# Attention planned with other durations for transfers, landings, query splits and GpSimd steps

## The chip, the cores and the metric

The kernel runs as one program on one core of one Trainium2 chip. The metric is the device time of one execution in microseconds (us), the median of several runs. Every tensor is fp32.

## The reference

Attention with a position bias from a small network, then a mixture of 8 experts of which each token takes 2, then a two-layer network with a cosine gate. Cut to what matters:

```python
# attention: B=2, H=8, S=576, D=64; hidden width 32 of the bias network
scores = q @ k.T / sqrt(D)
x = log1p(|i - j|) / log1p(max(i, 1))
bias = relu(x[..., None] @ w1 + b1) @ w2
attn = exp(scores + bias - max); attn /= sum + 1e-9
x = (attn @ v).transpose(0, 2, 1, 3).reshape(1152, 512)
# experts: 1152 tokens, top 2 of 8, 512 -> 1024 -> 512
noisy = x @ w_gate + log1p(exp(x @ w_noise)) * noise
out[mask] += top2_w[mask, k, None] * (relu(x[mask] @ w1[e]) @ w2[e])
# last stage: 512 -> 2048 -> 512
h = x @ w_in
return (h * cos(h)) @ w_out
```

## The kernel before

The program has two stages under one launch: attention with the routing of the tokens (0 to about 246 us of the span), and the experts with the last network (the rest). Matrix products keep fp32 exactness by splitting an operand in a rounded high part and a low part, so most products run twice.

**Attention** works in 72 steps. A step is one head of one block of 128 query rows. The first 8 steps are the block `it=4` (the last 64 rows of both batches), and steps 8 to 71 are `it=0` to `it=3` for either batch, 8 heads each. One step is: four score matmuls into `S` (L489, eight in the first block), a DVE operation that adds the bias and takes the row minimum (`ttr`, L494, which writes `t` and `m`), the exponential on ACT (L503), four transposes on PE (L510), and a copy `et` to SBUF (L275 on ACT or L277 on DVE). Every second step adds a transpose of the two 64-column tails (L522) and its copy `etl`, and the product with `vt` (`av`, L538). `S` has two buffers, so the scores of step n+2 wait for the `ttr` of step n.

Around that stand the jobs that feed it. `qjobs` (L289) loads a query block (L308), copies its high part (`qt`, L305 on ACT or L307 on DVE) and subtracts for the low part (L316, DVE). `kjobs` does the same for the keys (L329, low part L339 on DVE or GpSimd). `vjobs` loads the values, four transfers of 512 KB from L283. `bjobs` makes the bias of `it=4` and `it=0`: features (L381, L383), matmuls (L392), evacuations `bst` (L398 on ACT, L400 on DVE) and a transfer into the tile `bias` (L404). `bjobs2` makes the bias of `it=1` to `3` from the table `dtab` (loaded into the tile `kraw` at L926, scaled at L925), with features L428 and L430, matmuls L438, evacuations L448 and L450, a transfer to `dist` in DRAM (L458) and one back (L462). After the last head of a block the routing of its 128 tokens is worked out (a tile, 0 to 8; its one-hot and slot arithmetic on DVE between L786 and L857, its scatter on GpSimd).

**What sets the order.** Nothing is scheduled on the chip. Every operation is handed to `Plan.op` with the engines it may run on and a duration for each, a priority, and what it reads and writes. `Plan.run` (L67 on) simulates this with one clock per engine: it takes, among the operations that could start within 0.08 us of the earliest, the one of lowest priority, gives it to the engine where it would end soonest, and emits it. A transfer with `xfer` occupies one modelled DMA pipe for so long and counts as landed `land` us after that. So the numbers handed over decide both which engine does a piece of work and where it stands in that engine's queue. On the chip every engine works through its queue strictly in that order and waits where data are not there. SP issues all loads and stores of this stage from one queue too. The second stage has a plan of its own, with `land=2.3`.

The four `vt` transfers are planned together, after the last key loads (`after=[kl[...]]`), and every `av` reads all of `vt`.

Of the kernel before, what the change touches and what calls it, by code (L numbers as in the profile page):

```python
# [165 lines left out]
def attention_moe_cosine_mlp_kernel(  # L166
# [5 lines left out]
    nc = tc.nc  # L172
# [53 lines left out]
    with ExitStack() as actx:  # L226
# [39 lines left out]
        P = Plan(bufs, ("aux",))  # L266
# [20 lines left out]


        def qjobs(it, b, prio, after=()):  # L289
            key = (it, b)  # L290
            n = 128 if it < 4 else 64
            o = 0 if it < 4 else 64 * b

            def raw():
                return tl("qraw", key).bitcast(F32).rearrange("p h s -> p (h s)")[:, 0:H * n]

            def rows16():
                return raw().rearrange("p (h a r) -> p h a r", h=H, r=16)

            def part(u):  # L300
                return tl("qt", key)[:, u, :, o:o + n].rearrange("p h (r a) -> p h a r", r=16)

            def hi(e):
                if e == "ACT":
                    nc.scalar.activation(part(0), rows16(), AF.Copy)  # L305
                else:
                    nc.vector.tensor_copy(part(0), rows16())  # L307
            P.op({"SP": 0.45}, lambda e: nc.sync.dma_start(  # L308
                raw(), qd[b][:, it * 1024:it * 1024 + 8 * n]),
                prio - 3, w=[("qraw", key)], xfer=0.0115 * n, after=after)  # L310
# [15 lines left out]
        def kjobs(p, b, prio):  # L326
# [3 lines left out]
                           w=[("kraw", key)], xfer=0.82, after=late)  # L330
            for j in range(2):
# [11 lines left out]
                P.op({"DVE": 0.67, "POOL": 1.5}, lo, prio + 0.2, r=[("kraw", key), ("kt", key, j, 0)], w=[("kt", key, j, 1)])  # L343
# [21 lines left out]
        def bjobs(it, when):  # L365
            nA = 8 if it < 4 else 4
            for a in range(nA):
# [35 lines left out]
                for d in range(2 if it == 4 else 1):  # L403
                    bdma[a if it == 4 else 10 + a] = P.op({"SP": 0.625}, (lambda d, a, key: lambda e: nc.sync.dma_start(  # L404
                        spread(tl("bias", it), it, a, d), tl(*key)[:, 0:S]))(d, a, key),
                        pr + 0.2, r=[key + (0,), key + (1,)], w=[("bias", it, a, d)], xfer=0.82)
# [6 lines left out]
        def bjobs2(it, when):  # L413
            for a in range(8):
# [38 lines left out]
                for side in range(2):  # L453
# [7 lines left out]
                    w=[("dist", A)], xfer=0.85)  # L461
# [3 lines left out]
                    pr + 0.3, r=[("dist", A)], w=[("bias", it, a, 0)], xfer=0.82)  # L465
# [14 lines left out]
        def ajobs(n):  # L480
# [20 lines left out]
            qks[n] = P.op({"PE": 0.25 * 2 * len(bs)}, qk, n, r=nin, w=[("S", n)])  # L501
# [16 lines left out]
            P.op({"DVE": 0.1, "POOL": 0.34}, lambda e: (nc.gpsimd if e == "POOL" else nc.vector).tensor_copy(  # L518
# [20 lines left out]
            P.op({"PE": 1.34 if b is not None else 2.1}, av, n + 3, r=["v", ets[0], ets[1], el], w=[ax2], hold=[ok])  # L539
# [8 lines left out]
        def wjobs(i, pr):  # L548
            rk = ("raw", i)
            P.op({"SP": 0.45}, lambda e: nc.sync.dma_start(tl(*rk), mwp[i]), pr, w=[rk], xfer=1.46,  # L550
# [329 lines left out]
        def setup():  # L880
            P.op({"SP": 0.45}, dma(sm1, small1), -20, w=["sm1"], xfer=0.5)
            P.op({"SP": 0.45}, dma(w1l, ltab), -20, w=["w1l0"], xfer=1.64)
# [620 lines left out]
```

## Time and profile before

| | us |
|---|---|
| median of three runs | 681.82 |
| lowest, highest | 681.18, 684.20 |
| the profiled execution | 689.02 |
| its span (first to last instruction) | 687.2 |
| end of attention (last matmul of L657) | 245.88 |
| PE busy of the span | 632.1 (92%) |
| DVE busy of the span | 510.0 (74%) |

The profiled execution is 7.2 us longer than the median of the runs. Times below are positions in its span. PE is the busiest engine over the span. The rows that matter for this case come from the first 246 us.

### The profile page before, as it was taken

Reading aid. Unit: us, or ns where it says so; the run is one execution under the profiler, and the core shown is the slowest. Engines: PE = TensorE matmul, PEld = TensorE weight load, DVE = VectorE, ACT = ScalarE, POOL = GpSimd, SP = SyncE. Lnnn points to the kernel's source line nnn. Section 1 sums busy time; section 2 is a strip of 40 time slices with the busy share of each in tenths; the row PEclk is TensorE's granted clock in tenths of the full one; section 3 lists DMA queues with packets and bytes.
Section 4 is the critical chain, followed back from the end, with each engine's and each line's share of the span. In section 5 each row is a group of like instructions: output and inputs, shape, how many; then the busy total and the mean of one; then the engine's idle time right before and its main releaser. Section 6 shows DMA issues by size and latency. Waiting matters only on the chain.

```text
span 687.2 us, 12766 instructions
## 1 busy us (share of the span) xinstructions
PE 632.1 (92%) x4678; PEld 552.3 (80%) x4678; DVE 510.0 (74%) x1271; ACT 395.6 (58%) x791; POOL 107.1 (16%) x179
## 2 busy tenths in 40 slices
PE   5778998898899849999998998999999999999996
PEld 1346676675578649999998998999999999999996
DVE  6796897898878637989969888766998545554443
ACT  5666687777668525666645646544665444444333
POOL 4140124313222210002100011021400040001000
PEclk9998999999999959999999999999999999999999
DMA  5858788676658329698897897974730040001001
GB/s 174 207 162 255 247 281 270 214 217 199 204 165 267 106 73 279 189 302 269 238 301 211 250 281 207 250 201 157 240 100 25 0 138 1 1 7 40 1 1 46
DMA packets 58177, 116.45 MB, mean 169 GB/s; under 512 B 7024, under 2 KB 26864, under 8 KB 56048
## 3 DMA queue, kind: packets, MB, share of 16 engines
q1 hardware_dynamic: 54544, 104.41, 51.1%
q0 software_dynamic: 3552, 11.04, 4.8%
q8 instruction: 41, 0.67, 0.4%
q14 instruction: 40, 0.33, 0.2%
HBM read 78.12 MB, written 32.58 MB: 161 GB/s over the span
## 4 chain that ended last, share of the span: by engine, by line
PE 51%; DMA 6%; DVE 5%; issue 2%; ACT 1%; SPq 0%; DVEq 0%; POOL 0%; ACTq 0%
PE H L1002 25%; PE Y L1002 25%; DMA wraw<-in_mwp_dram 3%; DMA io<-xg 2%; DVE qt L1042 1%; DVE whl L1042 1%; DVE io L1153 1%; DMA xg<-x,token 1%; PE H L1191 1%; DMA bias<-xg 1%; DVE s L1072 1%; DVE s L1103 0%; ACT qt L1040 0%; DVE hhl L1133 0%; DVE qraw L1108 0%
## 5 line engine op out<-in xcount | busy, mean ns | idle before, releaser
L1002 PE MATMUL Y<-hhl,qt 128*128 128x304 f32 x468 | 73.3, 302 | 4.3 <-DVE hhl L1133 4.1
L1002 PE MATMUL Y<-w,hhl 128*128 128x512 f32 (+1 forms) x330 | 74.8, 372 | 0.0
L1002 PEld LDWEIGHTS Y<-hhl,qt 128*128 128x128 f32 x468 | 66.8, 188 | 5.6 <-DVE hhl L1133 5.5
L1002 PEld LDWEIGHTS Y<-w,hhl 128*128 128x128 f32 x330 | 56.7, 188 | 8.7
L503 ACT ACTIVATE e<-t,m 128x576 f32<-128x576 f32 x72 | 55.5, 771 | 11.8 <-DVE m L494 10.6
L489 PE MATMUL S<-kt,qt 128*128 128x288 f32 x320 | 59.0, 313 | 2.9 <-DVE m L494 2.9
L494 DVE CUSTOM_DVE_ANT_0 t<-S,bias 128x576 f32<-128x576 f32 x72 | 53.4, 750 | 9.4 <-DMA bias<-e 2.7
L1002 PE MATMUL H<-qraw,qt 128*128 128x304 f32 (+1 forms) x300 | 50.9, 321 | 8.3 <-issue 8.3
L1002 PEld LDWEIGHTS H<-qraw,qt 128*128 128x128 f32 x300 | 47.9, 199 | 9.1 <-issue 8.6
L489 PEld LDWEIGHTS S<-kt,qt 128*128 128x128 f32 x320 | 45.1, 190 | 8.5 <-DVE m L494 4.1
L1131 ACT ACTIVATE hhl<-H 128x304 fp32r<-128x304 f32 x64 | 26.7, 417 | 40.3 <-PE H L1002 38.4
L1002 PE MATMUL H<-qraw,w 128*128 128x384 f32 x264 | 49.3, 336 | 0.0
L1242 ACT ACTIVATE u<-H 128x384 f32<-128x384 f32 (+1 forms) x52 | 23.8, 466 | 42.2 <-PE H L1002 40.3
L1002 PEld LDWEIGHTS H<-qraw,w 128*128 128x128 f32 x264 | 46.6, 188 | 1.7
L510 PE MATMUL etp<-ident,e 128*128 128x128 f32 x288 | 44.6, 278 | 3.3 <-ACT e L503 2.6
L538 PE MATMUL aux<-et,vt 128*64 128x128 f32 (+1 forms) x640 | 42.5, 277 | 5.5 <-DMA vt<-in_vd_dram 3.2
L1042 DVE TENSOR_TENSOR qt<-wraw,qt 128x1024 fp32r<-128x1024 f32 x35 | 42.7, 1224 | 6.2 <-ACT qt L1040 5.6
L1002 PE MATMUL Y<-hhl,whl 128*128 128x304 f32 x300 | 45.6, 300 | 0.0
L1248 ACT ACTIVATE u<-u 128x384 f32<-128x384 f32 (+1 forms) x52 | 25.7, 498 | 34.1 <-DVE u L1246 33.8
L538 PEld LDWEIGHTS aux<-et,vt 128*64 128x64 f32 x640 | 33.2, 143 | 13.7 <-DMA vt<-in_vd_dram 3.5
L1254 DVE TENSOR_TENSOR hhl<-u,hhl 128x384 fp32r<-128x384 f32 (+1 forms) x52 | 27.2, 526 | 22.7 <-ACT hhl L1252 22.0
L1040 ACT ACTIVATE qt<-wraw 128x1024 fp32r<-128x1024 f32 x36 | 37.7, 1053 | 10.5 <-DMA wraw<-in_mwp_dram 6.1
(206 smaller groups left out, 1372.6 us busy)
## 6 DMA issues: line engine op xcount, KB each, us to landing
wraw<-in_mwp_dram SPq DMA_DIRECT2D x64, 512.0 KB
r<-in_mw2p_dram SPq DMA_DIRECT2D x16, 1024.0 KB
dist<-bst SPq DMA_DIRECT2D x24, 295.5 KB
bias<-dist SPq DMA_DIRECT2D x24, 288.0 KB
xg<-zero SPq DMA_DIRECT2D x20, 256.0 KB
yd<-zero SPq DMA_DIRECT2D x20, 256.0 KB
yd<-io SPq DMA_DIRECT2D x32, 160.0 KB
io<-xg SPq DMA_DIRECT2D x28, 160.0 KB
```

Source lines behind the costliest of these rows:

```text
L489: nc.tensor.matmul(s[:, hf, 0:HF], tl("qt", (it, bb))[:, u, h, :], kt[:, bb, h, hf * HF:hf * HF + HF], start=(i == 0), stop=(i == len(term ...
L494: nc.vector.tensor_tensor_reduce(out=tl("t", n).rearrange("p (a j) -> p a j", a=2), in0=tl("S", n)[:, :, 0:HF], in1=tl("bias", it)[:, h, : ...
L503: P.op({"ACT": 0.76}, lambda e: nc.scalar.activation(tl(*ek)[:, 0:S], tl("t", n), AF.Exp, bias=tl("m", n), scale=-1.0, accum_out=tl("rs", ...
L510: nc.tensor.transpose(tl("etp", n)[:, j * 128:(j + 1) * 128], tl(*ek)[:, j * 128:(j + 1) * 128], ident)
L538: nc.tensor.matmul(tl(*ax2)[h0, q0], lw, rx, start=(s == 0), stop=(s == 4))
L1002: nc.tensor.matmul(out_, lw(a), rx(b_), start=(first and i == 0), stop=(last and i == n - 1))
L1040: P.op({"ACT": 0.947}, lambda e: nc.scalar.activation(wt(i)[:, 0], tl(*rk), AF.Copy), pr, r=[rk], w=[wname(i) + (0,)])
L1042: P.op({"DVE": 1.135, "POOL": 2.4}, lambda e: (nc.gpsimd if e == "POOL" else nc.vector).tensor_tensor(wt(i)[:, 1], tl(*rk), wt(i)[:, 0].bi ...
L1131: P.op({"ACT": 0.053 + 0.00083 * W}, lambda en: nc.scalar.activation(tl(*hk)[:, 0, 0:W], tl(*pk)[:, 0:W], AF.Relu), g + 0.3, r=ks, w=[hk + ...
L1242: P.op({"ACT": 0.06 + 0.00083 * m}, lambda e: nc.scalar.activation(u(), h(), AF.Copy, scale=1.0 / (2.0 * math.pi), bias=0.25), z, r=ks, w= ...
L1248: P.op({"ACT": 0.187 + 0.00083 * m}, lambda e: nc.scalar.activation(u(), u(), AF.Sin, scale=2.0 * math.pi), z + 0.04, r=[un[1]], w=[un[2]])
L1254: P.op({"DVE": 0.069 + 0.00104 * m}, lambda e: nc.vector.tensor_tensor(part(1), u(), part(0).bitcast(F32), op=OP.subtract), z + 0.07, r=[u ...
```

## The change

Only numbers that the attention plan is fed are changed, and none of the code that an operation emits. Transfers get longer times, a landed transfer counts 2.0 us after its pipe time where it was 1.25 us, the query split costs become larger on either engine (high part for 128 rows: ACT 0.92 to 1.90 us, DVE 0.60 to 0.94; low part on DVE 1.14 to 2.01), and two GpSimd steps, the scores and the products with `vt` get other durations. The `av` of the first block falls from 2.1 to 1.4 us.

```diff
-        P = Plan(bufs, ("aux",))
+        P = Plan(bufs, ("aux",), land=2.0)
...
+        QA, QD, QL = 0.0144, 0.0068, 0.0152
...
-                prio - 3, w=[("qraw", key)], xfer=0.0115 * n, after=after)
+                prio - 3, w=[("qraw", key)], xfer=0.0133 * n, after=after)
...
-            P.op({"ACT": 0.0067 * n + 0.06, "DVE": 0.0042 * n + 0.065}, hi, prio + 0.1, r=[("qraw", key)],
+            P.op({"ACT": QA * n + 0.06, "DVE": QD * n + 0.065}, hi, prio + 0.1, r=[("qraw", key)],
                  w=[("qt", key, 0)])
-            P.op({"DVE": 0.0084 * n + 0.065}, lambda e: nc.vector.tensor_tensor(
+            P.op({"DVE": QL * n + 0.065}, lambda e: nc.vector.tensor_tensor(
...
-                           w=[("kraw", key)], xfer=0.82, after=late)
+                           w=[("kraw", key)], xfer=1.17, after=late)
...
-                P.op({"DVE": 0.67, "POOL": 1.5}, lo, prio + 0.2, ...
+                P.op({"DVE": 0.68, "POOL": 1.65}, lo, prio + 0.2, ...
...
-                     xfer=1.46, after=[kl[tuple(VAF[s])]] if VAF[s] else [])
+                     xfer=1.7, after=[kl[tuple(VAF[s])]] if VAF[s] else [])
...
-            P.op({"PE": 1.34 if b is not None else 2.1}, av, n + 3, ...
+            P.op({"PE": 1.38 if b is not None else 1.4}, av, n + 3, ...
```

In the same way the transfers of `bias` go from 0.82 to 1.18, of `dist` from 0.85 to 1.01, of the first expert weights from 1.46 to 1.7 and of the feature table from 1.64 to 2.08; scores go from 0.25 to 0.265 per batch and half, and the GpSimd copy of a tail from 0.34 to 0.40.

The emitted instructions are the same kinds in nearly the same number, in another order and partly on another engine, and only in the attention stage. Of the eight high parts of queries with 128x1024 elements, ACT copies 6 before and 1 now, DVE 2 and 7. Copies `et` go from 14 to 12 on DVE, tail copies of scores from 14 to 13, output copies from 10 to 8, and ACT takes these. Of the low parts of the keys GpSimd takes 8 where it took 9. Lines from 287 on have a number that is one higher in the changed kernel.

**Place 1, start of the stage.** The queue of SP, from the next to last key load on, before:

```order
L329 DMA kraw<-in_kd_dram 128x576
L404 DMA bias<-bst 16x8x576 x2
L329 DMA kraw<-in_kd_dram 128x576
L404 DMA bias<-bst 16x8x576
L283 DMA vt<-in_vd_dram 128x1024 x4
L926 DMA kraw<-in_dtab_dram 128x512
L404 DMA bias<-bst 16x8x576
L308 DMA qraw<-in_qd_dram 128x1024 x2
```

And after:

```order
L330 DMA kraw<-in_kd_dram 128x576
L405 DMA bias<-bst 16x8x576
L330 DMA kraw<-in_kd_dram 128x576
L405 DMA bias<-bst 16x8x576
L283 DMA vt<-in_vd_dram 128x1024 x4
L405 DMA bias<-bst 16x8x576
L927 DMA kraw<-in_dtab_dram 128x512
L309 DMA qraw<-in_qd_dram 128x1024 x2
L405 DMA bias<-bst 16x8x576
```

The four `vt` transfers stand behind the sixth `bias` transfer of `it=0` instead of the seventh, and the eighth has gone behind the two query loads.

DVE at the same place before, from the evacuation ahead of the first query block of `it=0` on (`ISA t,m` is the `ttr` of step 4):

```order
L400 TENSOR_SCALAR bst<-aux,sm_73 128x288
L307 CAST qt<-qraw 128x8x8x16
L383 TENSOR_SCALAR feat<-w1l,sm_73 128x576
L316 TENSOR_TENSOR qt<-qraw,qt 128x8x8x16
L494 ISA t,m<-S,bias 128x576
L494 ISA m 128x1
L277 CAST kt<-kraw 64x576
L400 TENSOR_SCALAR bst<-aux,sm_73 128x288
```

And after:

```order
L277 COPY et<-etp 128x512
L495 ISA t,m<-S,bias 128x576
L495 ISA m 128x1
L308 CAST qt<-qraw 128x8x8x16
L384 TENSOR_SCALAR feat<-w1l,sm_73 128x576
L317 TENSOR_TENSOR qt<-qraw,qt 128x8x8x16
L277 CAST kt<-kraw 64x576
L401 TENSOR_SCALAR bst<-aux,sm_73 128x288
```

The `ttr` of step 4 has moved ahead of the query split.

**Place 2, the first steps of `it=2`.** PE before, from the scores of step 41 on:

```order
L489 MATMUL S<-kt,qt 128x288 x4
L510 MATMUL etp<-ident,e_2125 128x128 x4
L438 MATMUL aux<-feat,sm_73 32x400 x4
L522 MATMUL aux<-ident,e_2095 128x128
L489 MATMUL S<-kt,qt 128x288 x8
L510 MATMUL etp<-ident,e_2234 128x128 x4
```

And after, from the same scores:

```order
L490 MATMUL S<-kt,qt 128x288 x4
L539 MATMUL aux<-et,vt 64x128 x8
L539 MATMUL aux<-etl,vtl 64x128 x2
L439 MATMUL aux<-feat,sm_73 32x400 x4
L511 MATMUL etp<-ident,e_2168 128x128 x4
L523 MATMUL aux<-ident,e_2086 128x128
L539 MATMUL aux<-et,vt 64x128 x8
L539 MATMUL aux<-etl,vtl 64x128 x2
L439 MATMUL aux<-feat,sm_73 32x416 x4
L719 MATMUL aux<-ot,sm_74 32x128 x4
L737 MATMUL aux<-ident,ot 128x128 x4
L490 MATMUL S<-kt,qt 128x288 x8
```

Between the scores of step 41 and of step 42 stand two `av`, two bias matmuls and the first part of a routing tile; before there were one set of transposes, one bias matmul and a tail.

**Place 3, the routing of the last tile but one.** DVE before, from the `ttr` of step 71 on:

```order
L559 TENSOR_TENSOR qt<-wraw,qt 128x512 x2
L797 TENSOR_SCALAR rt<-rt 128x2
L799 TENSOR_TENSOR rt<-rt 128x1
L824 ISA rt<-oh,aux 128x8
L824 ISA rt 128x1
L824 ISA rt<-oh,aux 128x8
L824 ISA rt 128x1
L277 COPY et<-etp 128x512
L828 TENSOR_TENSOR rt<-rt 128x2
```

And after:

```order
L798 TENSOR_SCALAR rt<-rt 128x2
L800 TENSOR_TENSOR rt<-rt 128x1
L495 ISA t,m<-S,bias 128x576
L495 ISA m 128x1
L560 TENSOR_TENSOR qt<-wraw,qt 128x512 x2
L825 ISA rt<-oh,aux 128x8
L825 ISA rt 128x1
L825 ISA rt<-oh,aux 128x8
L825 ISA rt 128x1
L856 TENSOR_SCALAR rt<-rt 128x1
L829 TENSOR_TENSOR rt<-rt 128x2
```

The copy `et` has gone from the middle of this arithmetic (to ACT), and the two small steps for the weights stand ahead of the `ttr`.

## Rows read from the trace of the kernel before

**Rows 1.** Windows: stretch, length, busy PE, PEld, DVE, ACT, POOL, clock, DMA, GB/s
```profile
40.00:49.00 9.00, 6.71 (x56) 3.89 (x53) 8.94 (x14) 6.55 (x13) 5.01 (x4) 1.00 0.35 98
49.00:54.00 5.00, 4.10 (x34) 2.87 (x31) 4.87 (x8) 2.44 (x5) 1.27 (x2) 1.00 0.85 279
54.00:61.00 7.00, 3.77 (x41) 2.97 (x41) 1.67 (x7) 1.69 (x4) 0.25 (x2) 0.85 1.04 306
61.00:66.00 5.00, 5.00 (x65) 4.22 (x62) 4.07 (x10) 4.61 (x8) 0.00 (x0) 0.52 0.71 253
...
66.00:229.00 163.00, 151.28 (x1566) 112.96 (x1564) 140.10 (x526) 122.57 (x293) 43.84 (x115) 1.00 0.70 218
120.00:160.00 40.00, 35.30 (x361) 25.92 (x361) 36.10 (x145) 28.89 (x69) 11.89 (x31) 1.00 0.69 216
```

**Rows 2.** Timeline of PE, start of the stage: start, us, what, wait ahead
```profile
48.41 1.10 PE L392 MATMUL aux<-feat,sm 128*32 128x288 f32 x6 [1.63 <-DVE bst L400]
...
57.08 0.34 PE L538 MATMUL aux<-et,vt 128*64 128x64 f32 x4 [0.76 <-DMA vt<-in_vd_dram]
59.89 0.48 PE L538 MATMUL aux<-et,vt 128*64 128x64 f32 x4 [2.48 <-DMA vt<-in_vd_dram]
...
62.17 1.12 PE L538 MATMUL aux<-et,vt 128*64 128x64 f32 x16
...
66.98 0.69 PE L538 MATMUL aux<-et,vt 128*64 128x64 f32 x16
```

**Rows 3.** Timeline of SP's queue, the same stretch
```profile
48.42 0.54 SPq L404 DMA_DIRECT2D bias<-bst  x1
49.01 2.15 SPq L283 DMA_DIRECT2D vt<-in_vd_dram  x4
51.81 0.33 SPq L926 DMA_DIRECT2D kraw<-in_dtab_dram  x1
```

**Rows 4.** Timeline of DVE, the same stretch
```profile
42.78 1.09 DVE L307 CAST qt<-qraw 128x1024 fp32r<-128x1024 f32 x1
43.71 0.49 DVE L383 TENSOR_SCALAR feat<-w1l,sm 128x576 f32<-128x576 f32 x1
44.12 2.15 DVE L316 TENSOR_TENSOR qt<-qraw,qt 128x1024 fp32r<-128x1024 f32 x1
46.12 0.75 DVE L494 CUSTOM_DVE_ANT_0 t<-S,bias 128x576 f32<-128x576 f32 x1
...
47.84 0.52 DVE L400 TENSOR_SCALAR bst<-aux,sm 128x288 f32<-128x288 f32 x1
...
60.67 0.49 DVE L925 TENSOR_SCALAR kraw<-kraw,sm 128x512 f32<-128x512 f32 x1 [4.24 <-DMA kraw<-in_dtab_dram]
```

**Rows 5.** Timeline of ACT, the exponential of step 4
```profile
46.97 0.78 ACT L503 ACTIVATE e<-t,m 128x576 f32<-128x576 f32 x1 [0.80 <-DVE m L494]
```

**Rows 6.** Timeline of PE and DVE at the first steps of it=1 and it=2
```profile
100.73 0.77 PE L438 MATMUL aux<-feat,sm 128*32 128x336 f32 x8
...
111.63 0.75 DVE L494 CUSTOM_DVE_ANT_0 t<-S,bias 128x576 f32<-128x576 f32 x1
...
156.33 0.76 DVE L494 CUSTOM_DVE_ANT_0 t<-S,bias 128x576 f32<-128x576 f32 x1 [0.76 <-DMA bias<-dist]
...
157.15 1.49 PE L489 MATMUL S<-kt,qt 128*128 128x288 f32 x8 [1.33 <-DVE m L494]
```

**Rows 7.** Groups by line and shape, 0 to 246 us: count, busy, mean ns
```profile
L305 ACT ACTIVATE qt<-qraw 128x1024 fp32r<-128x1024 f32 x6 | 12.7, 2116 | 0.6 <-PE S L489 0.4
...
L277 DVE COPY et<-etp 128x512 f32<-128x512 f32 x14 | 9.5, 680 | 0.1
...
L307 DVE CAST qt<-qraw 128x1024 fp32r<-128x1024 f32 x2 | 2.2, 1106 | 0.0
```

**Rows 8.** Timeline of DVE and PE at the end of the stage
```profile
229.86 0.69 DVE L277 COPY et<-etp 128x512 f32<-128x512 f32 x1
...
254.18 2.11 PE L1002 MATMUL H<-qraw,qt 128*128 128x304 f32 x7 [8.31 <-issue]
```

More of the change, by code (lines that the diff above doesn't have):

```diff
@@ L342, in kjobs @@
                 P.op(cost(S, False), hi, prio + 0.1, r=[("kraw", key)], w=[("kt", key, j, 0)])
-                P.op({"DVE": 0.67, "POOL": 1.5}, lo, prio + 0.2, r=[("kraw", key), ("kt", key, j, 0)], w=[("kt", key, j, 1)])
+                P.op({"DVE": 0.68, "POOL": 1.65}, lo, prio + 0.2, r=[("kraw", key), ("kt", key, j, 0)], w=[("kt", key, j, 1)])
         def knames(p, b):
@@ L405, in bjobs @@
                         spread(tl("bias", it), it, a, d), tl(*key)[:, 0:S]))(d, a, key),
-                        pr + 0.2, r=[key + (0,), key + (1,)], w=[("bias", it, a, d)], xfer=0.82)
+                        pr + 0.2, r=[key + (0,), key + (1,)], w=[("bias", it, a, d)], xfer=1.18)
         dist = {}
@@ L460, in bjobs2 @@
                     tl("bst", key)[:, 0:591]))(A, key), pr + 0.2, r=[("bst", key, 0), ("bst", key, 1)],
-                    w=[("dist", A)], xfer=0.85)
+                    w=[("dist", A)], xfer=1.01)
                 P.op({"SP": 0.625}, (lambda A, a: lambda e: nc.sync.dma_start(
@@ L464, in bjobs2 @@
                     dist[A][15:15 + 128 * BW].rearrange("(r h w) -> r h w", r=16, h=8)[:, :, 0:S]))(A, a),
-                    pr + 0.3, r=[("dist", A)], w=[("bias", it, a, 0)], xfer=0.82)
+                    pr + 0.3, r=[("dist", A)], w=[("bias", it, a, 0)], xfer=1.18)
         def bnames(it):
@@ L500, in ajobs @@
             nin = [x for bb in bs for x in qnames(it, bb) + knames(h // 2, bb)]
-            qks[n] = P.op({"PE": 0.25 * 2 * len(bs)}, qk, n, r=nin, w=[("S", n)])
+            qks[n] = P.op({"PE": 0.265 * 2 * len(bs)}, qk, n, r=nin, w=[("S", n)])
             P.op({"DVE": 0.67}, ttr, n + 0.5, r=[("S", n)] + bnames(it), w=[("t", n), ("m", n)])
@@ L517, in ajobs @@
             e0 = ("e0", n // 2)
-            P.op({"DVE": 0.1, "POOL": 0.34}, lambda e: (nc.gpsimd if e == "POOL" else nc.vector).tensor_copy(
+            P.op({"DVE": 0.1, "POOL": 0.4}, lambda e: (nc.gpsimd if e == "POOL" else nc.vector).tensor_copy(
                 tl(*e0)[:, S:S + 64], tl(*ek)[:, 512:S]), n + 1.5, r=[ek], w=[e0 + ("tail",)], shy={"DVE": 0.6})
@@ L538, in av @@
                             nc.tensor.matmul(tl(*ax2)[h0, q0], lw, rx, start=(s == 0), stop=(s == 4))
-            P.op({"PE": 1.34 if b is not None else 2.1}, av, n + 3, r=["v", ets[0], ets[1], el], w=[ax2], hold=[ok])
+            P.op({"PE": 1.38 if b is not None else 1.4}, av, n + 3, r=["v", ets[0], ets[1], el], w=[ax2], hold=[ok])
             P.op(cost(128), lambda e: cp(tl(*ok)[:, p, :], tl(*ax2)[:, 0:128], e), n + 3.2, r=[ax2], w=[ok + (p,)])
@@ L549, in wjobs @@
             rk = ("raw", i)
-            P.op({"SP": 0.45}, lambda e: nc.sync.dma_start(tl(*rk), mwp[i]), pr, w=[rk], xfer=1.46,
+            P.op({"SP": 0.45}, lambda e: nc.sync.dma_start(tl(*rk), mwp[i]), pr, w=[rk], xfer=1.7,
                  after=[qks[min(int(pr), NS - 1)]])
@@ L881, in setup @@
             P.op({"SP": 0.45}, dma(sm1, small1), -20, w=["sm1"], xfer=0.5)
-            P.op({"SP": 0.45}, dma(w1l, ltab), -20, w=["w1l0"], xfer=1.64)
+            P.op({"SP": 0.45}, dma(w1l, ltab), -20, w=["w1l0"], xfer=2.08)
             P.op({"DVE": 0.7}, lambda e: nc.vector.tensor_scalar(w1l, w1l, w1c, None, op0=OP.mult), -20,
```

## The prediction

> **What bounds the kernel now.** I read the table of windows first. From 66 to 229 us PE is busy 151.28 of 163 us and DVE 140.10 [rows 1]: PE sets the pace there, with DVE not far behind, and from 120 to 160 us DVE is even the fuller one (36.10 of 40 against 35.30). The start is another matter. From 40 to 54 us DVE is full (8.94 of 9, 4.87 of 5) and PE waits for it; from 54 to 61 us nearly everything stands still: PE 3.77 of 7, DVE 1.67, ACT 1.69, while the DMA engines are at 1.04 of their share [rows 1]. Just before, from 40 to 49 us, those same DMA engines are at 0.35. So transfers that could have run in the idle stretch are bunched in the next one.
>
> Next I read the timelines of the start for what ends each wait. PE has two waits for `vt`, 0.76 and 2.48 us, and goes on at 59.89 [rows 2]. DVE waits 4.24 us for the table `dtab`, until 60.67 [rows 4]. SP's queue says why both are late: `vt` is issued at 49.01, right behind the seventh `bias` transfer at 48.42, and `dtab` at 51.81 behind `vt` [rows 3]. That `bias` transfer waits for the evacuation that DVE does from 47.84 to 48.36 [rows 4], and SP issues in order. Nothing that `vt` itself needs is late; it is queued behind something that is.
>
> The waits have a second price. In the window 61 to 66 us the granted clock is 0.52, the lower of the two levels (1.2 GHz), and it is 1.00 from 66 us on [rows 1]; 16 `av` matmuls take 1.12 us at 62.17 and 0.69 us at 66.98 [rows 2].
>
> **The change part by part.** The profiled execution is 689.02 us for a span of 687.2; I make the sum against it and carry the difference over to the median of the runs, 681.82. The rows are about 1% long for that, which is nothing beside the bounds.
>
> *`vt` one place earlier.* It now waits behind the sixth `bias` transfer. That hangs on an ACT evacuation that stands behind the exponential of step 4 (46.97 [rows 5]), and so on the `ttr` of step 4. This `ttr` has moved ahead of the query split on DVE: by starts, 46.12 − 42.78 = 3.34 us for the copy, a feature and the subtraction [rows 4]. The exponential could begin at 43.6, end with the rest of its operation near 44.6, the evacuation near 45.1, and `vt` go out near 45.8 instead of 49.01: −3.2 us. If ACT finds other work ahead of it, or the sixth bias matmul waits for a feature, it is less; below nothing it can't be, since the seventh transfer is behind it in either order.
>
> *What PE makes of it.* The last part of `vt` would be there at 59.89 − 3.2 = 56.7. PE reaches its first `av` some 0.7 earlier (one copy `et` of 680 ns [rows 7] is now behind the `ttr` of step 7, on which the scores ahead of `av` hang), so it would wait some 0.7 us instead of 0.76 + 2.48 = 3.24. PE: −3.2 us, bounds −1 (the transfer shares the DMA engines with others and comes hardly earlier) and −3.9.
>
> *What DVE makes of it.* The seventh `bias` transfer still waits for the same evacuation, since the work ahead of it on DVE is the same in another order, so `dtab`, now right behind that one alone, goes out near 49.0 instead of 51.81: −2.8, and the 4.24 us of idle time shrink to near 1. But then the order has two things that DVE did not have there: a tail copy that waits for PE to get through four sets of `av`, 1.3 to 3.3 us of waiting by whether these run at the upper or lower clock level, and both query copies, 2 × 1106 ns where ACT did one in 2116 [rows 7]. Against the 4.24 and the 0.9 us that it waited for ACT's copy, DVE comes out 0 to 1.9 us ahead.
>
> So PE is 3.2 us ahead after the start and DVE some 1. In 66 to 229 us PE has 11.7 us free and DVE 22.9 [rows 1], so DVE can catch up over the first steps; I take −3.2 for the start, the PE row being the nearest, with −1.0 (DVE's lead alone) and −5.4 (below) as ends.
>
> *The loop.* At step 40 the `ttr` waited for its last bias rows, 0.76 us, and PE then 1.33 us [rows 6]. Now about 13.8 us of PE work stand between the last bias matmul of that block and the scores of step 42, where it took 13.2 with the wait in it: −1.3. At step 24 it is the other way. The last bias matmul runs at 100.73 and the `ttr` begins at 111.63 [rows 6], 10.9 us later, and ends 0.75 after that. The PE work between that matmul and the scores that wait for this `ttr` is about 11.1 us now, so a wait of about 0.8 us appears: +0.8. Together −0.5, bounds −1.5 and +2.
>
> *Five query copies from ACT to DVE.* 5 × 1.106 = 5.5 us more on DVE, less two copies `et` (1.4 us [rows 7]) and some bias evacuations and small copies that go to ACT. Between 0 (all beside PE work) and +4.1 on the path. ACT is freed of about 5 × 2.1 us, but is not what PE mostly waits for. DVE has 22.9 us free in the loop, but only 3.9 of 40 from 120 to 160 us [rows 1]. I take +0.5.
>
> *The end.* The copy `et` of 0.69 us at 229.86 [rows 8] stood in the chain that leads from the last tile but one to its scatter, its reload and PE's last work of the stage; it is gone from there: −0.7, bounds −1.5 and 0 if PE gets there no sooner. The 8.31 us between the stages [rows 8] stay: nothing of them changes. The second stage's own order is the same.
>
> Sum: −3.2 − 0.5 + 0.5 − 0.7 = −3.9, so 689.02 becomes 685.1, and the median 681.82 becomes 677.9.
>
> **The rivals.**
>
> *The half-clock stretch goes too.* At 48.41 PE goes on after a wait of 1.63 us, and the clock of that window is still 1.00 [rows 1, 2]; the fall came behind two waits of 3.24 us in sum. With 0.7 left, the clock may stay up. From about 60 to 66 us the matmuls would take 0.69/1.12 of their time: 5.9 × 0.38 = −2.2 more. That gives 675.7. Against it: DVE is only 0 to 1.9 us ahead, and PE can't go far without its `ttr`. The Trainium skill, page "TensorE: Matmul & The Clock Gate", section "Part 1: The HAM clock gate", says that the lower rate is the default and that sustained activity releases it; by that rule a start without the gap would bring this rival's time, and the traces agree as far as the clock here fell behind a gap.
>
> *DVE takes it back.* PE's lead ends at the first step for which DVE is late, and DVE's lead is what counts, with about −1 of it left: −1.0 − 0.5 + 0.5 − 0.7 = −1.7, so 680.1. For it: the `ttr` of steps 8 and 9 now stand behind the copies and a bias evacuation. Against it: DVE's 22.9 us of free time.
>
> *`vt` does not go out earlier.* Then the order of the sixth transfer's own feeders (features on DVE, an evacuation on ACT behind its features) is what holds SP, and only loop and end remain: −0.7, so 681.1.
>
> *Slower: the copies sit where DVE is the bound.* Counted along the order, DVE has 2.5 to 3 us more work ahead of the `ttr` of steps 40 to 44 than before, in the stretch in which it is 90% busy [rows 1]. If all of the 4.1 us are on the path there, nothing of the 1.3 comes back at step 40, the wait of 0.8 at step 24 is real, and DVE's lead from the start is 0, then +4.1 + 0.8 − 0.7 = +4.2: 686.0. It decides from the point at which DVE's free time ahead of step 40 is less than the copies need.
>
> **How the numbers follow.** The forecast 677.9 gets 0.40, the half-clock rival (675.7) 0.17, DVE's give-back (680.1) 0.21, `vt` no earlier (681.1) 0.08, the slower one (686.0) 0.14. The range goes from 673.5 (the half-clock rival with the other terms at their better ends) to 685.0, which leaves out most of the slower rival and a little below. 0.5% is 3.4 us, about what a measurement of this kernel tells from no change: faster is below 678.4, slower above 685.2. The forecast's own spread, about 675.5 to 680, puts some 0.28 of its 0.40 in faster; with the half-clock rival and a little of the others that is 0.47. Slower gets 0.14 with a little for what I have not seen, 0.15, and the rest is 0.38.
>
> **What would show it.** In the trace of the changed kernel: `vt` issued near 46 and `dtab` near 49; PE's waits for `vt` below 1 us in sum; DVE's scaling of the table near 58; the clock in the window 61 to 66 us tells the forecast from the half-clock rival. PE should have no wait at the scores of step 42, and a new one of some 0.8 us at step 26. The first matmul of the second stage, at 254.18 before [rows 8], should stand near 250.3. If `vt` goes out at 48 or later, the first step is wrong; if it goes out at 46 and the second stage still begins past 252, DVE took it back; if waits for a `ttr` behind a query copy between 120 and 160 us grow by several us, the slower rival holds.

## The result

The changed kernel takes 677.09 us in the median of 20 runs (674.13 to 682.65), the kernel before, measured beside it, 684.28 us in the median of 20 runs (678.47 to 690.47). The ratio is 0.9916, 95% interval 0.989 to 0.9941, or about −5.7 us, between −7.5 and −4.0. (The ratio compares fast runs alone; the two medians as they stand are 7.2 us apart, which the interval holds.) The forecast was faster by 3.9 us, to 677.9. That 677.09 lies so near 677.9 is chance: the forecast started from 681.82, the median of three runs, and 20 runs have 684.28. What can be compared is −3.9 with −5.7. The profiled execution of the changed kernel is 676.62 us, its span 674.8.

The start of the stage after, first SP's queue, then DVE's `ttr` of step 4 and the scaling of the table, then PE's first `av` (they answer to [rows 3], [rows 4] and [rows 2]):

```profile
44.85 0.54 SPq L405 DMA_DIRECT2D bias<-bst  x1
45.44 2.13 SPq L283 DMA_DIRECT2D vt<-in_vd_dram  x4
48.81 0.54 SPq L405 DMA_DIRECT2D bias<-bst  x1
49.74 0.33 SPq L927 DMA_DIRECT2D kraw<-in_dtab_dram  x1
```

```profile
42.72 0.75 DVE L495 CUSTOM_DVE_ANT_0 t<-S,bias 128x576 f32<-128x576 f32 x1
...
58.65 0.48 DVE L926 TENSOR_SCALAR kraw<-kraw,sm 128x512 f32<-128x512 f32 x1
```

```profile
55.73 0.79 PE L490 MATMUL S<-kt,qt 128*128 128x288 f32 x4 [0.27 <-DVE m L495]
56.45 0.69 PE L539 MATMUL aux<-et,vt 128*64 128x64 f32 x16
```

The four `vt` transfers go out at 45.44 instead of 49.01, behind the sixth `bias` transfer at 44.85, and the table at 49.74 instead of 51.81. The wait for the table (4.24 us) is gone, and PE has no wait for `vt`. The windows that answer to [rows 1]:

```profile
54.00:61.00 7.00, 6.73 (x104) 5.69 (x102) 3.97 (x12) 3.43 (x9) 0.24 (x1) 1.00 1.04 306
61.00:66.00 5.00, 4.46 (x87) 3.05 (x85) 4.29 (x8) 2.99 (x8) 0.00 (x0) 1.00 0.21 78
66.00:225.00 159.00, 151.36 (x1538) 113.02 (x1535) 141.10 (x538) 119.64 (x302) 48.38 (x120) 1.00 0.73 230
120.00:160.00 40.00, 37.47 (x384) 26.46 (x383) 36.59 (x140) 28.47 (x74) 11.67 (x29) 1.00 0.71 217
```

From 54 to 61 us PE is busy 6.73 of 7 us (3.77 before), and the granted clock is 1.00 in 61 to 66 us, where it was 0.52. In the loop PE is busy 151.36 of 159 us (151.28 of 163 before).

The end of the stage. Each pair of rows is the last block of matmuls of the stage and the first of the next, the first pair before, the second after. The first start is that block's, the second that of the second stage, and the bracket the idle time between.

```profile
243.82 2.06 PE L657 MATMUL S<-ident 128*128 128x128 f32 x8
254.18 2.11 PE L1002 MATMUL H<-qraw,qt 128*128 128x304 f32 x7 [8.31 <-issue]
```

```profile
233.78 2.05 PE L658 MATMUL S<-ident 128*128 128x128 f32 x8
241.90 4.39 PE L1003 MATMUL H<-qraw,qt 128*128 128x304 f32 x16 [6.06 <-issue]
```

The second stage begins 12.28 us earlier (241.90 against 254.18), which is just the difference of the two spans, 12.4. That is twice what the comparison of many runs gives. So the two traces can't be taken as they stand: the one of before shows an execution of 689.02 us, over the median of its runs, and the one of after an execution near its median. The first experiment is on that.

### The profile page after: what moved, and what is told of

Its sections match the earlier page's. It is cut to its first block, busy times and chain, and to the rows that moved or that the text cites. A ratio compares the mean times of both kernels' runs of the same rounds, so it can differ in the third digit from the quotient of the medians.

```text
span 674.8 us, 12762 instructions
## 1 busy us (share of the span) xinstructions
PE 627.9 (93%) x4678; PEld 549.8 (81%) x4678; DVE 509.5 (75%) x1267; ACT 390.5 (58%) x797; POOL 108.0 (16%) x177
## 4 chain that ended last, share of the span: by engine, by line
PE 40%; DMA 11%; DVE 10%; issue 3%; SPq 2%; ACT 1%; DVEq 0%; ACTq 0%
PE H L1003 19%; PE Y L1003 19%; DMA io<-xg 7%; DVE qt L1043 2%; DVE s L1104 2%; DMA wraw<-in_mwp_dram 2%; SPq L1095 1%; DMA yd<-io 1%; DVE io L1154 1%; DVE hhl L1134 1%; DVE whl L1043 1%; DVE s L1073 1%; DMA xg<-x,token 1%; DVE xnext L1109 1%; PE H L1192 1%
## 5 line engine op out<-in xcount | busy, mean ns | idle before, releaser
L504 ACT ACTIVATE e<-t,m 128x576 f32<-128x576 f32 x72 | 55.5, 772 | 14.4 <-DVE m L495 11.2
L490 PEld LDWEIGHTS S<-kt,qt 128*128 128x128 f32 x320 | 45.4, 190 | 7.8 <-issue 4.1
L1003 PEld LDWEIGHTS Y<-hhl,whl 128*128 128x128 f32 x300 | 42.7, 188 | 2.3 <-DVE hhl L1134 1.8
L1041 ACT ACTIVATE qt<-wraw 128x1024 fp32r<-128x1024 f32 x36 | 37.8, 1054 | 11.1 <-DMA wraw<-in_mwp_dram 7.3
L1245 DVE TENSOR_SCALAR s<-u 128x384 f32<-128x384 f32 (+1 forms) x52 | 18.1, 351 | 33.7 <-ACT u L1243 33.7
```

The source lines that it names most:

```text
L490: nc.tensor.matmul(s[:, hf, 0:HF], tl("qt", (it, bb))[:, u, h, :], kt[:, bb, h, hf * HF:hf * HF + HF], start=(i == 0), stop=(i == len(term ...
L504: P.op({"ACT": 0.76}, lambda e: nc.scalar.activation(tl(*ek)[:, 0:S], tl("t", n), AF.Exp, bias=tl("m", n), scale=-1.0, accum_out=tl("rs", ...
L1003: nc.tensor.matmul(out_, lw(a), rx(b_), start=(first and i == 0), stop=(last and i == n - 1))
L1041: P.op({"ACT": 0.947}, lambda e: nc.scalar.activation(wt(i)[:, 0], tl(*rk), AF.Copy), pr, r=[rk], w=[wname(i) + (0,)])
L1245: P.op({"DVE": 0.069 + 0.00052 * m}, lambda e: nc.vector.tensor_scalar(k(), u(), MAGIC, MAGIC, op0=OP.add, op1=OP.subtract), z + 0.01, r=[ ...
```

## The experiments

Apart from the second trace of each kernel, every experiment is a list of the stage's operations in a chosen order, with the engine of each, put in the place of what the planner works out. With the list of the kernel before it is instruction for instruction that kernel, and likewise for the changed one, so that any part of either order can be taken alone. The diffs show what moves in such a list. Ratios are to the kernel before on the same chip. These runs carry the number of their chip: 5 for the first four experiments below (up to the two halves), 11 for the changed order with the old end, for the two that move `total_i` and the slots, and for the changed kernel once more, 0 for the other four. The first two traces, before and after, carry none. The kernel before has a median of 683.73 us on chip 5, 683.77 on 11 and 690.16 on 0, so times of chip 0 are not to be set beside those of the other two. The changed kernel itself was not run on chip 0; what was run there can be compared with it by the ratios alone.

### The kernel before once more

> The kernel before once more, for a second trace of it. Two questions: which of the waits of the first trace belong to the order of the instructions, and which to the one execution. If the wait for vt (0.76 and 2.48 us) and the half-rate stretch from 59 to 65 us belong to the order, they stand again within 0.5 us, vt goes out within 0.5 us of 49.0 and the second stage begins near 254. If the difference between the two first traces (254.18 against 241.90 us for the first matmul of the second stage) was partly one slow execution of before, this trace begins the second stage several us earlier, near 248, and the waits in it that have shrunk are the ones that vary.

One execution, 677.66 us, span 675.8, the second stage from 245.03 us on. That is as untypical as the first trace: the 29 runs of this kernel beside it lie between 679.30 and 687.43. SP's `vt`, DVE's scaling of the table, PE's first `av`, and the windows:

```profile
48.89 2.14 SPq L283 DMA_DIRECT2D vt<-in_vd_dram  x4
51.70 0.33 SPq L926 DMA_DIRECT2D kraw<-in_dtab_dram  x1
```

```profile
58.37 0.49 DVE L925 TENSOR_SCALAR kraw<-kraw,sm 128x512 f32<-128x512 f32 x1 [0.44 <-DMA kraw<-in_dtab_dram]
```

```profile
57.36 0.69 PE L538 MATMUL aux<-et,vt 128*64 128x64 f32 x16
```

```profile
49.00:54.00 5.00, 4.09 (x20) 2.18 (x19) 4.30 (x7) 2.40 (x5) 0.94 (x1) 0.66 0.91 302
54.00:61.00 7.00, 7.00 (x107) 6.18 (x106) 4.50 (x12) 3.83 (x10) 0.48 (x2) 1.00 1.02 355
61.00:66.00 5.00, 3.63 (x56) 2.39 (x57) 4.14 (x7) 5.00 (x11) 0.57 (x1) 1.00 0.48 166
```

`vt` goes out at the same time, 48.89, and PE has no wait for it; DVE waits 0.44 us for the table instead of 4.24. Two things differ. The data came earlier: the table is scaled 2.30 us sooner (58.37 against 60.67), and the first `av`, done by 58.05, finds all of `vt`, whose last part came at 59.89 in the first trace. And PE asked later: it reaches its first `av` at 57.36 instead of 55.87. For the half-rate stretch is not gone, it stands earlier: the clock is 1.00 from 54 to 66 us, but 0.66 in 49 to 54, where the first trace has 1.00 [rows 1]. So of the 3.24 us of waiting 1.49 were hidden by a PE that was late itself. Other waits differ too. The `ttr` ahead of that of step 28, in the first trace and in this one:

```profile
119.35 0.76 DVE L494 CUSTOM_DVE_ANT_0 t<-S,bias 128x576 f32<-128x576 f32 x1 [2.09 <-PE etp L510]
```

```profile
114.94 0.74 DVE L494 CUSTOM_DVE_ANT_0 t<-S,bias 128x576 f32<-128x576 f32 x1
```

The wait of 2.09 us in the first is absent in the second. Step 68 is reached at 220.41 in the first trace and at 211.41 in the second, 9 us apart with the same instructions. Most of that may be the chip and not the execution: from the `ttr` of step 12 to that of step 68 the first trace takes 143.0 us, the four traces on chip 0 take 141.6 to 144.5, and the eight on chips 5 and 11 take 136.4 to 139.5, whatever their order; the first trace of the changed kernel takes 137.6. So the two first traces look like two different chips, which nothing here can confirm. Either way a row of a wait in one trace is a price of that execution. The waits of 3.24 us and the half-rate stretch at this place, on which most of the forecast stood, do not come in every execution. The traces with `vt` issued between 48.6 and 49.7 show PE waiting for it 3.24, 0, 1.17, 1.23, 0.80, 0 and 2.31 us, those with `vt` at 47.3 or earlier not at all in seven traces. Nor is a wait of 0 a gain by itself. Of the two traces of the old start on chip 11 (`total_i` and `slots` below) one reaches its first `av` at 58.66 us and waits for nothing, its clock 0.57 in 49 to 54 us; the other reaches it at 55.51, waits 2.31 us, and goes on at 58.61. Their rows, and the windows of the one that waits, which has the lower clock level in part again:

```profile
58.66 0.69 PE L542 MATMUL aux<-et,vt 128*64 128x64 f32 x16
```

```profile
56.48 0.34 PE L542 MATMUL aux<-et,vt 128*64 128x64 f32 x4 [0.51 <-DMA vt<-in_vd_dram]
58.61 0.34 PE L542 MATMUL aux<-et,vt 128*64 128x64 f32 x4 [1.80 <-DMA vt<-in_vd_dram]
```

```profile
54.00:61.00 7.00, 4.69 (x64) 3.77 (x64) 2.46 (x8) 2.44 (x6) 0.24 (x1) 0.89 1.02 332
61.00:66.00 5.00, 4.58 (x67) 3.12 (x63) 4.06 (x7) 4.97 (x11) 0.00 (x0) 0.81 0.49 186
```

### `vt` alone

```diff
 SP  bias transfer of it=0, the sixth
+SP  vt x4
 SP  bias transfer, the seventh
-SP  vt x4
 SP  dtab
```

> The kernel before in its own order, written out as a list, with one thing moved: the four vt transfers stand ahead of the seventh bias transfer of it=0 in SP's queue. Theory one (the start carries the gain, because vt was queued behind a transfer that is late): vt goes out near 45, PE's waits for vt fall from 3.24 to below 0.5 us, the clock stays at its upper level, and the time is 3 to 5 us lower, a ratio of 0.993 to 0.996. Theory two (what is won at the start is taken back by DVE, and the gain of the change comes from the order of the loop): the waits go just the same, but the time moves by less than 1.5 us, a ratio of 0.998 to 1.0.

Ratio 0.9941, interval 0.9915 to 0.9968: −4.0 us (−5.8 to −2.2). `vt` goes out at 44.77, no wait for it is left, and the clock is 1.00 from 40 to 66 us. Theory one holds for the old order. The 12 runs lie between 677.9 and 684.5.

### The two halves: start, and the rest

```diff
 order of the operations up to the scores of step 10
-  as before
+  as in the changed kernel
 all others: as before
```

> The order of the changed kernel up to the scores of step 10, then what is left in the order of the kernel before. Theory one (the start): nearly the whole gain of the change, a ratio of 0.991 to 0.994. Theory two (the loop): a ratio of 0.997 to 1.0.

Ratio 0.9993, interval 0.9966 to 1.0021. No gain, against theory one. The reason stands in the trace at the seam. PE waits, in the steps right behind it:

```profile
71.14 0.80 PE L493 MATMUL S<-kt,qt 128*128 128x288 f32 x4 [0.44 <-DVE m L498]
...
73.73 0.66 PE L740 MATMUL aux<-ident,ot 128*128 128x128 f32 x4 [1.44 <-DVE bst L454]
...
76.22 0.47 PE L735 MATMUL aux<-ident,lgs 128*128 128x128 f32 x1 [1.39 <-ACT lgs L279]
```

and DVE ahead of the second of them:

```profile
70.33 0.74 DVE L498 CUSTOM_DVE_ANT_0 t<-S,bias 128x576 f32<-128x576 f32 x1
...
71.01 2.09 DVE L320 TENSOR_TENSOR qt<-qraw,qt 128x1024 fp32r<-128x1024 f32 x1
73.03 0.65 DVE L454 TENSOR_SCALAR bst<-aux,sm 128x432 f32<-128x432 f32 x1
```

The new start leaves a subtraction of a query block (2.09 us, L320 in this file) and a bias evacuation undone. The old rest has them in a row on DVE, ahead of what PE asks for next: 0.44, 1.44 and 1.39 us of waits that the changed kernel doesn't have there. Behind them the clock is at its lower level for most of the next window, where the two traces of the changed kernel have 1.00 at this place:

```profile
75.00:82.00 7.00, 5.78 (x26) 4.15 (x27) 4.57 (x14) 3.40 (x9) 1.07 (x4) 0.52 0.82 293
```

The half is not the start alone; it is the start with a seam.

The other half has its diff the other way round, old up to step 10 and new from there:

> The other half: the order of the kernel before up to the scores of step 10, then what is left in the order of the changed kernel. Theory one (the start): a ratio of 0.997 to 1.0, since only the 1.33 us at step 40 and the 0.69 us at the end are won and some 0.8 us at step 24 lost. Theory two (the loop): 0.991 to 0.995. If the sum of this gain and that of the run with only the start is well over the gain of the change, the halves are not independent.

Ratio 0.9955, interval 0.9925 to 0.9985, between the two theories. In its trace `vt` goes out at 48.83 and PE waits 1.17 us for it. Half of the gain is there without the new start. The run contains the new end as well as the new loop, so it doesn't tell these two apart. The two halves together bring 0.5 + 3.1 = 3.6 of the 5.7 us: less than the whole, not more.

### `vt` back to its old place in the changed order

```diff
 SP  bias transfer of it=0, the sixth
-SP  vt x4
 SP  bias transfer, the seventh
+SP  vt x4
 SP  dtab
```

> The order of the changed kernel with one thing moved back: the four vt transfers stand behind the seventh bias transfer of it=0 in SP's queue, as before. The second trace of the kernel before had no wait for vt at all though it went out at 48.89, so the wait is one of some executions only. Theory one (the early vt is worth its median of -4 us as in the run that moved vt alone, by taking these executions away): a ratio to before of 0.995 to 0.998, half of the gain lost. Rival (the changed order does not hang on vt any more, because av begins at 56.45 instead of 55.87 and its other waits are late anyway): 0.990 to 0.993, as the changed kernel.

Ratio 0.9905, interval 0.9873 to 0.9936: the whole gain of the changed kernel, the rival's number. SP and PE in its trace:

```profile
49.52 2.12 SPq L287 DMA_DIRECT2D vt<-in_vd_dram  x4
51.76 0.55 SPq L930 DMA_DIRECT2D kraw<-in_dtab_dram  x1
```

```profile
55.81 0.80 PE L493 MATMUL S<-kt,qt 128*128 128x288 f32 x4 [0.26 <-DVE m L498]
...
57.90 0.34 PE L542 MATMUL aux<-et,vt 128*64 128x64 f32 x4 [0.80 <-DMA vt<-in_vd_dram]
```

`vt` goes out at 49.52, and PE waits 0.80 us, once. So the early `vt`, worth 4.0 us in the old order, is not what the changed kernel lives on; the two intervals leave it some 2 us at most there (an estimate from both, and across two chips). Its scores of step 9 run at 55.81, as in the changed kernel (55.73). What in the new order makes a late `vt` harmless I have not separated. The windows have one candidate: from 40 to 49 us, with the clock at 1.00 in all traces, PE is busy 8.00 to 8.44 us in the six traces with the new start, this one among them, and 6.38 to 6.71 us in the eight with the old one. With the `ttr` of step 4 ahead of the query split, PE gets its next work there sooner.

### The query copies back on ACT

```diff
 six query copies qt (high part), same places in the order
-  on DVE
+  on ACT
```

> The order of the changed kernel with the six query copies that went from ACT to DVE (one of them of the first block) back on ACT, at the same places of the order. It prices the move. If the copies on DVE cost 0.5 us as the forecast has it, the ratio to before is 0.990 to 0.992. If they cost the 4 us of the slower rival, it is 0.985 to 0.988. If ACT's 2.1 us copies hold up exponentials and copies that PE waits for, it is 0.993 to 0.997.

Ratio 0.9916, interval 0.9882 to 0.995, the same as with the copies on DVE. On the same chip the run before this one, with the copies on DVE and a late `vt`, has a median of 683.05 us and this one 683.80. A cost or a gain of the move isn't told from nothing; the intervals leave room for some 3 us either way, and so for the 0.5 us too, but not for the 4 us of the slower rival.

### The end of the stage

```diff
+PE   counts of tile 8
 PE   transposes of the reloaded rows (L589)
-PE   counts of tile 8, among these
 DVE  total (difference of the counts)
-DVE  low part of the first expert's rows
-DVE  maximum
-DVE  low part
-DVE  total_i
-DVE  slots and weights of tile 8
+DVE  maximum, slots, total_i, weights of tile 8
+DVE  low part x2
```

The counts on PE move too, and with them a small ACT step (L819): DVE's sum and slots hang on the counts, so the new end is not a matter of DVE alone. PE's counts and `total_i`, before and after:

```profile
242.02 0.19 PE L815 MATMUL aux<-oh,ones 128*128 128x8 bf16 x2
244.65 0.16 DVE L853 CAST total_i<-total 128x9 int32<-128x9 f32 x1
```

```profile
229.65 0.19 PE L816 MATMUL aux<-oh,ones 128*128 128x8 bf16 x2
230.74 0.17 DVE L854 CAST total_i<-total 128x9 int32<-128x9 f32 x1
```

Against the start of PE's last block (243.82 and 233.78) `total_i` comes 0.83 us later before and 3.04 us earlier after.

The first run has the changed kernel's order from step 71 on, and the old order ahead of that:

> The order of the kernel before up to the scores of step 71, then what is left in the order of the changed kernel: only the routing of the last two tiles and the first expert's low parts stand in the new order, with the sum total_i and the slots of tile 8 ahead of the low parts. In the traces with the old end the second stage begins 10.4 to 11.1 us after PE begins its last matmuls of the first stage, in the two with the new end 8.1 and 8.2 us. Theory (the end is worth these 2.5 us): a ratio of 0.995 to 0.998, and a gap of 8 to 8.4 us in the trace. Rival (the gap is shorter because something else, such as the transfers, stood differently): a gap of 10 us or more and a ratio of 0.999 to 1.001.

Ratio 0.9952, interval 0.9921 to 0.9984: −3.3 us (−5.5 to −1.1). From the start of PE's last block to the start of the second stage it is 7.40 us, by these rows:

```profile
243.56 2.05 PE L661 MATMUL S<-ident 128*128 128x128 f32 x8
250.96 5.41 PE L1006 MATMUL H<-qraw,qt 128*128 128x304 f32 x20 [5.35 <-issue]
```

The opposite, the changed order with the old end:

> The order of the changed kernel up to the scores of step 71, then what is left in the order of the kernel before. Theory (the new end is worth about 2.5 us or more, and is half of the whole gain): the gap from PE's last block of matmuls of the first stage to the second stage is 10 to 11 us in the trace instead of 8.1, and the ratio to before is 0.994 to 0.997. Rival (the gain lies in start and loop): 0.990 to 0.993, as the changed kernel.

```profile
232.98 2.05 PE L661 MATMUL S<-ident 128*128 128x128 f32 x8
243.57 6.31 PE L1006 MATMUL H<-qraw,qt 128*128 128x304 f32 x30 [8.54 <-issue]
```

The gap is 10.59 us, as the theory has it. But the ratio is 0.992, interval 0.9889 to 0.9952, where the changed kernel in the same comparison has 0.9914: the old end costs 0.4 us there by the medians of the ratios, with an interval that also takes in 2. The gap overstates it, since with the old end PE gets to its last block sooner. From the `ttr` of step 68 to the second stage the traces with the old end take 33.77, 33.62, 33.13, 33.68 and 32.99 us, those with the new end 31.49, 31.38, 31.34, 31.17, 30.54, 31.92 and 32.24: 2.0 us less in the mean. Part of that is the order ahead of it: steps 68 to 71 alone take 6.2 to 6.3 us in the new order and 7.3 to 7.6 in the old one. With the same order ahead of it, the new end is worth 1.5 us in the old order (33.55 to 32.08 in the mean) and 1.8 in the new one (32.99 to 31.18; on chip 11 alone 32.99 to 31.38).

Which part of the end it is, the next two were to tell, from the kernel before:

```diff
 first run: DVE  maximum and total_i
+  ahead of both low parts
-  among them
 second run: DVE  slots and weights of tile 8
+  ahead of both low parts
-  behind them
```

> The kernel before with two small DVE instructions moved: the maximum and the integer copy total_i, on which every engine branches between the stages, stand ahead of the two low parts (2 x 0.68 us) instead of among them; the slots of tile 8 stay behind them. Theory A (the branch waits for total_i): the gap falls to 8 to 9 us and the ratio is 0.996 to 0.998. Theory B (it is the scatter of tile 8, which GpSimd starts once the slots are there, or what comes behind it): the gap stays 10 to 11 us, the ratio 0.999 to 1.001.

> The other half of the new end: in the kernel before the slots and weights of tile 8 stand ahead of the two low parts on DVE, and total_i stays among them, and so some 0.5 us later than before. Theory A (the branch waits for total_i): the gap stays 10 to 11 us, the ratio 0.999 to 1.002. Theory B (the scatter of tile 8): GpSimd starts the scatter some 2 us earlier against PE's end, the gap falls to 8 to 9 us and the ratio is 0.996 to 0.998. If neither of the two runs shortens the gap, it takes both.

Ratios 1.0016 (0.9985 to 1.0048) and 1.0026 (0.9994 to 1.0057). Neither alone brings anything in the time. The gaps are 9.58 and 11.44 us: the first is below the 10.4 to 11.1 of the old end, but not at the 8 to 9 of theory A; the second is no shorter. From step 68 to the second stage the traces take 32.08 and 34.74 us. Both runs leave PE's counts behind the reload, so neither could bring `total_i` or the slots out as early as the new end does: with `total_i` moved it comes 0.42 us ahead of PE's last block, in the seven traces with the new end 1.7 to 3.2 us ahead. Either it takes both, or the earlier counts, or the rest of the new end (the copy `et` out of the chain, the order ahead of it) matters more. That stays open. What fits `total_i` is that from its start to the second stage all fourteen traces take 9.5 to 11.2 us.

### Start and end without the loop

```diff
 SP  vt x4 ahead of the seventh bias transfer, as above
 from the scores of step 71 on: as in the changed kernel
 the rest: as before
```

> The kernel before with vt moved ahead of the seventh bias transfer and with the new end, the loop left as it was. If start and end are the whole gain and add up, the ratio is 0.989 to 0.993, that of the changed kernel. If the new order of the loop carries a part of its own, it is 0.993 to 0.996.

Ratio 0.9927, interval 0.989 to 0.9964. The product of the two single ones is 0.9941 × 0.9952 = 0.9893. The interval holds that, and the changed kernel's number, and the bound of the other theory. It is no better than the changed kernel, so the `vt` move and the new end in the old order reach about the same as all of the new one. That fits the traces, in which the loop gains nothing by the new order: from step 12 to step 68 it takes 136.35, 137.15, 137.27 and 137.46 us with the old loop on chips 5 and 11 (without the run with the seam), and 137.42, 137.57, 137.62 and 137.64 with the new one (the 137.62 is the first trace after, which carries no chip number).

### The changed kernel once more

> The changed kernel once more, on the chip of the three others, so that old end and new end under the changed order are compared on one chip, and for a second trace of it. Ratio 0.989 to 0.994. In the trace vt goes out near 45.4 and PE has no wait for it, and the gap between the stages is near 8.1 us. Theory of the margin (the early vt takes away slow executions rather than a fixed time): the spread of its runs is narrower than that of before.

Ratio 0.9914, interval 0.9885 to 0.9943; its 12 runs lie between 674.62 and 681.97, the 35 of before on that chip between 678.56 and 688.44. That is narrower, as the theory of the margin has it, but 12 runs are set against 35. No wait for `vt` again, though it went out at 47.24 this time and not near 45.4, with the whole start 1.8 to 2.7 us later. Nor is the start free of the lower clock here: it is 0.58 in 28 to 36 us, 0.78 in 49 to 54 and 0.91 in 54 to 61. The gap at the end is 8.20 us (236.23 to 244.43). Step 68 is reached at 213.05, against 210.41 in the first trace.

## Why the prediction was right, and where it was not

**`vt` one place earlier: right.** Forecast 45.8, measured 45.44 (47.24 in the second trace); the `ttr` of step 4 at 42.72, where the sum had 42.78 for it. The time of this one move in the old order is −4.0 us, where the start was put at −3.2. In the new order moving it back cost nothing that could be told, so there the gain of the start doesn't hang on it, as the sum had it.

**What PE makes of it: the sum held, a step in it did not.** PE was to reach its first `av` 0.7 us earlier and wait 0.7. It reached it 0.58 later, at 56.45, and waited for nothing. And the 3.24 us were taken as a fixed price. Other traces of the same start have 0, 1.17, 1.23, 0 and 2.31, and the two zeros come with a PE that is itself late by the clock. The size that came out right is a mean over executions, which one trace could not give: that is luck.

**The half-clock stretch: the rival is not shown.** In the first trace after there is no gap, and the clock is 1.00 from 40 to 66 us (0.79 in 28 to 36, where the first trace of before has 1.00). But the stretch is a matter of the execution, and it moves. In the second trace of before PE waits 1.65 us at 48.30 and 0.91 us at 50.31, as in the first (1.63 at 48.41, 0.90 at 50.42); in 49 to 54 us the clock is 0.66 in the one and 1.00 in the other. The second trace of the changed kernel has 0.78 and 0.91 in 49 to 54 and 54 to 61 us without any wait for `vt`, and the run with only `total_i` moved has 0.57 and 0.82 there, with PE busy 7.00 of 7 us in the second window. The Trainium skill, page "TensorE: Matmul & The Clock Gate", section "Part 1: The HAM clock gate", has the lower rate as the default that activity releases. Two traces agree, in that those with 0.52 and 0.81 in 61 to 66 us have a gap of PE of 2.5 and 1.8 us just before; in the others a gap of this kind doesn't tell whether the clock falls.

**What DVE makes of it: right in its parts.** The table went out at 49.74 (forecast near 49.0) and was scaled at 58.65 (near 58). DVE waited 0.71 us for PE ahead of a tail copy, less than the 1.3 to 3.3 of the sum, and did both query copies in 2.09 us.

**The loop: +0.5 us instead of −0.5, by the means of the traces above (137.06 and 137.56 us from step 12 to step 68).** The wait at the scores of step 42 fell from 1.33 to 0.20 us and a new one of 0.60 came at step 26, where 0.8 was forecast. (The prediction's own terms, 10.9 + 0.75 − 11.1, give 0.55 and not 0.8; and the 1.33 was in part a price of that execution, 0.55 in the second trace of before.) But each has a companion that the sum did not have:

```profile
105.35 1.09 PE L539 MATMUL aux<-et,vt 128*64 128x128 f32 x16 [0.87 <-ACT bst L449]
...
108.30 0.66 PE L737 MATMUL aux<-ident,ot 128*128 128x128 f32 x4 [0.62 <-ACT lgs L275]
...
109.66 1.48 PE L490 MATMUL S<-kt,qt 128*128 128x288 f32 x8 [0.60 <-DVE m L495]
```

```profile
147.10 1.12 PE L539 MATMUL aux<-et,vt 128*64 128x128 f32 x16 [0.55 <-DVE bst L451]
...
150.82 0.66 PE L737 MATMUL aux<-ident,ot 128*128 128x128 f32 x4 [1.18 <-DVE bst L451]
151.68 1.48 PE L490 MATMUL S<-kt,qt 128*128 128x288 f32 x8 [0.20 <-DVE m L495]
```

In front of step 26 PE waits 0.87 and 0.62 us for ACT (a bias evacuation, the copy `lgs`), where it had 0.65 and 0.26 before; in front of step 42 for DVE's bias evacuations 0.55 and 1.18 us, where it had no other wait. PE's work was counted about right: from the last bias matmul of the block (96.31 and 135.62) to these scores, less the waits shown, it is 11.3 and 14.1 us, where the sum had 11.1 and 13.8. But the engines that feed it had moved as well, and the `ttr` came 12.5 us behind that bias matmul at step 24, where the sum had 10.9. All of the waits shown stand within 0.01 us in the second trace of the changed kernel, so they do belong to the order.

**Five query copies: not told from 0, nor from +0.5.** The run that took them back has the same ratio, to some 3 us. The slower rival, for which they were the price with 4.1 us, falls with that.

**The end: mis-sized, by a sentence that was wrong.** The term was −0.7, and "the 8.31 us between the stages stay: nothing of them changes". They became 6.06, and from step 68 to the second stage the new end takes 1.5 to 1.8 us less with the same order ahead of it. By the runs it is 3.3 us (5.5 to 1.1) in the old order, and 0.4 us in the changed one, not told apart from 2. The order showed that PE's counts of tile 8 had moved ahead of the reload, and `total_i` and the slots ahead of the low parts. The step that failed was to look only at PE's own last matmul, and not at the other engines that have to be through before the second stage begins.

**The sum.** −5.7 us (−7.5 to −4.0) against −3.9. In the traces, step 68 is reached at 220.41, 211.41, 219.04, 213.90 and 213.90 with the old start and loop, mean 215.7, and at 210.41, 213.05 and 210.58 with the new, mean 211.3. But the 219.04 is from chip 0, and the 220.41 has a loop as long as the traces there (that the rows are "about 1% long for that, which is nothing beside the bounds" was wrong). Without these two it is 213.1 against 211.3: −1.7, and −1.5 to −1.8 for the end. That makes −3.2 to −3.5, a little short of the measured interval, from six executions that differ by 3.5 us among themselves, so it is no proof. By these traces the start gains (the `ttr` of step 12 comes at 76.6 us in the mean of the six with the old start, 73.8 in the five with the new one, the run with the seam left out; chip 0 doesn't stand out there), the loop doesn't, the end gains more than the forecast gave it, and the errors of the terms in part cancel. The parts don't add up as single causes: `vt` alone gives −4.0 in the old order and nothing that can be told in the new one. Which part of the new start makes the order hold without the early `vt` is open.

## What to carry to other kernels

Take a second trace of the same kernel, on a chip that you know, before pricing a wait on a transfer: at equal issue times it was 3.24 us in one and 0 in the other, and a move that gives the transfer 3.5 us of margin then earns a mean, not the row. A wait of 0 may only say that the engine that asks was late itself. A fixed issue order is one piece: its start put ahead of another order's rest gained nothing, because the rest had its own work placed for another start. At a border between stages, count every engine's last instructions, and what they hang on, not only the last ones of the engine that sets the pace.

## What was not expected of the hardware

The same start with `vt` issued at 48.65 to 49.65 us made PE wait between 0 and 3.24 us for it. Part of that is when the data came (the table, right behind `vt`, was scaled at 58.37 in one execution and at 60.67 in another), part is when PE asked (first `av` between 55.51 and 58.66 us). The lower clock came at different places with the same instructions and nearly the same waits: 0.66 in 49 to 54 us in one trace of before, 0.52 in 61 to 66 in the other. The runs of before spread over 12.0 us, those of after over 8.5. One chip ran the kernel before in 690.16 us in the median, two others in 683.73 and 683.77, all three with a mean granted clock of 0.97 to 0.99 in these runs. The price of a query copy of 128x1024 is 2116 ns on ACT and 1106 to 1148 ns on DVE, and moving six of them from one to the other changed nothing that could be measured.
